# A chain of attention and two MLPs on one core: the up product of batch 1's channel MLP in Strassen's seven block products

## The chip, the core and the metric

The kernel runs on one core of a Trainium2 chip. The metric is the device time of one execution in microseconds (us). TensorE (PE in the profile) multiplies, its weight loads (PEld) lie beside its matmuls; VectorE (DVE), ScalarE (ACT) and GpSimd (POOL) do the rest, and SyncE (SP) issues most DMAs. Each engine takes its instructions in a fixed order.

## What is computed

The reference is an attention with cluster masks, then a channel MLP behind a mixing by Fourier transforms, then a gated MLP. The change touches the channel MLP alone:

```python
def _moe_ref(x, w_ch1, w_ch2) -> np.ndarray:
    X = np.fft.fft(x, axis=1)
    X = np.fft.fft(X, axis=2)
    mixed = np.real(X).astype(np.float32)
    u = x + mixed
    mu = np.mean(u, axis=-1, keepdims=True)
    var = np.mean((u - mu) ** 2, axis=-1, keepdims=True)
    un = (u - mu) / np.sqrt(var + 1e-06)
    ch = np.maximum(un @ w_ch1, 0.0) @ w_ch2
    return (u + ch).astype(np.float32)
```

Here x is 2 batches of 768 tokens with 512 features, w_ch1 is 512 x 2048 and w_ch2 2048 x 512. The gated MLP behind it (512 to 1024 and back, with a convolution over tokens and a sigmoid) runs in the same loop style with "second weights".

## The kernel before

**Number format.** Values of fp32 accuracy are held as two fp16 tiles, a high part and a low part (value less high part). A product takes three matmul passes, high x high, high x low and low x high (`pass3`, lines 490 to 493). The weights come as 64-bit numbers; `load_w` (line 725) fetches a block of 128 hidden features by an SP DMA into one of two raw buffers, `from64` (line 701) turns it into fp32 on VectorE and ScalarE, and the split gives the four pieces (up high and low, down high and low).

**The channel MLP.** It runs in blocks f = 0 to 15 of 128 hidden features, batch g = 0 first, then g = 1 (main loop, lines 1820 to 1849). `mlp1_up` (line 1647) makes block f + 1: for each half of the tokens (384) `up_half` sums 4 chunks of 128 input features by 3 passes, 12 matmuls into one of two PSUM banks called up; ScalarE writes the high part (line 1661), VectorE the low part (line 1663). Then `down` (line 1702) adds block f into six accumulator banks, one for each token tile of 128: 18 matmuls of 512 columns. So the up product of the next block always lies between a block's end and its use.

**Beside it.** A generator `side` is advanced once or twice inside each `down`. In batch 0 it is `later`: the mixing and the norm of batch 1 (`norm`, line 653), whose `swap` turns normed tiles by four transposes into an up bank, and whose results are the batch's activations `un`. In batch 1 it is `gate_in(0)` (line 1727): `measure` scales rows of U, then six token tiles are turned through an up bank (line 1771) into x, the gated MLP's input, one tile in each of f = 2 to 7. The loads of the second weights (blocks wb0 to wb7) are placed at the blocks of `B_LOADS` in batch 1; each takes the SBUF slot of a first weight block that its last down has freed. `scales("b")` after f = 12 forms their scales, and `split_16` the pieces of the first three.

**Order.** The instruction order of each engine is fixed at build time by a scheduler that goes by the written order and by when it expects an instruction to be ready. An accurate general version follows behind a flag that a set of checks computes; the profiled execution doesn't run it.

Of the kernel before, what the change touches and what calls it, by code (L numbers as in the profile page):

```python
# [2 lines left out]

# [6 lines left out]
F16 = mybir.dt.float16  # L10
# [438 lines left out]
def tile_net(ctx, tc, qk, v, cen, w12, w34, conv, dft, odd, out, general):  # L449
# [51 lines left out]
    def mixing(b, bank, bank2, low, other, rest):  # L501
# [223 lines left out]
    def load_w(k, f):  # L725
# [29 lines left out]
    def scales(k):  # L755
# [9 lines left out]
        V.tensor_reduce(sc[:, 0:2], o.rearrange("p (a f) -> p a f", a=2), AX.X, ALU.max)  # L765
        if k == "a" and not general:
# [29 lines left out]
    def heads_fit():  # L796
        o = up_bank("heads")
        least, most = (V_LEAST ** 2 * 128 * S, V_MOST ** 2 * 128 * S)
        V.tensor_scalar(hsum[:, 0:16], hsum[:, 0:16], QK_MOST ** 2, None, ALU.is_le)
        T.matmul(o[:, 0:24], ones.to_broadcast([128, 128]), hsum, start=True, stop=True)  # L800
        T.matmul(o[:, 32:40], ones.to_broadcast([128, 128]), ties, start=True, stop=True)
# [899 lines left out]

    def down(s, g, f, side, when=(2,)):
        w, h = ws.pop((s, g, f)), hs.pop((s, g, f))
# [3 lines left out]
        for t in range(NT):  # L1707
# [4 lines left out]
            if f == last:  # L1712
# [6 lines left out]
                else:  # L1719
# [74 lines left out]
    def later():  # L1794
# [25 lines left out]
    for g in range(B):  # L1820
        for f in range(16):
            if (g, f) < (B - 1, 15):
                mlp1_up(*((g, f + 1) if f < 15 else (g + 1, 0)))
            if (g, f) == (B - 1, 15):
                next(side, None)
            down(0, g, f, side, (1, 4) if g == 0 and f else (2,))
            for i in A_LOADS[f] if g == 0 else ():
# [15 lines left out]
            if (g, f) == (1, 12):  # L1843
# [104 lines left out]
```

## Time and profile before

| | us |
|---|---|
| median of 3 runs | 634.34 (633.04 to 634.71) |
| profiled execution | 634.69 |
| its span | 632.9 |
| TensorE busy | 608.3 |
| batch 1's first up matmul to the first matmul of the gated MLP | 363.36 to 494.90 |

The span is the time from the first to the last instruction; 1.8 us of the profiled execution lie around it. TensorE's granted clock is 1.00 in the stretches from 217 to 495 us. A busy time counts what the engine executes; what matters for an engine's worth is whether TensorE waits for it.

### The profile page before, as it was taken

The page shows a single profiled execution, that of the slowest core. Times are in us where ns is not written, and L with a number is a line of the kernel's source. Part 1 is how long each engine was busy: PE and PEld are TensorE (multiplying, and loading weights), DVE is VectorE, ACT ScalarE, POOL GpSimd, SP SyncE. Part 2 cuts the span into 40 slices and gives each one's busy share as a digit, 9 for nine tenths or more (in the row PEclk, how much of TensorE's full clock was granted, in tenths as well). Part 3 has the DMA queues.
Part 4 walks back from the last instruction along what each step waited for, and adds up shares of the span by engine and source line. Part 5 has one row for each costly group of instructions (what it writes and reads, how often), then busy time and mean ns, then how long its engine had stood idle before and what let it go on. Part 6 is the DMA issues. An engine that isn't in the chain of part 4 may idle for free.

```text
span 632.9 us, 11869 instructions
## 1 busy us (share of the span) xinstructions
PE 608.3 (96%) x4753; PEld 371.0 (59%) x4753; DVE 472.6 (75%) x784; ACT 413.0 (65%) x714; POOL 169.3 (27%) x137
## 2 busy tenths in 40 slices
PE   8899899999999999999999999999999999999995
PEld 4476577676877755566555555555555545555552
DVE  5989979899898889877894177777114599777663
ACT  6788899996889866873686134555115568866652
POOL 4978877875697300000200000000000000000000
PEclk9999999999999999999999999999999999999998
DMA  4676764641410513430353002333100003345102
GB/s 157 204 183 209 211 153 127 156 121 46 105 42 4 200 61 123 151 132 1 146 187 134 1 1 92 117 131 112 50 1 2 0 2 99 101 150 184 67 1 105
DMA packets 21945, 64.40 MB, mean 102 GB/s; under 512 B 7127, under 2 KB 8823, under 8 KB 19065
## 3 DMA queue, kind: packets, MB, share of 16 engines
q1 hardware_dynamic: 20872, 59.81, 30.0%
q0 software_dynamic: 1008, 3.75, 2.0%
q8 instruction: 39, 0.64, 0.4%
q14 instruction: 26, 0.20, 0.1%
HBM read 49.59 MB, written 4.89 MB: 86 GB/s over the span
## 4 chain that ended last, share of the span: by engine, by line
PE 68%; DVE 16%; ACT 11%; issue 2%; DMA 1%; DVEq 0%; ACTq 0%
PE acc L491 7%; PE acc L493 7%; PE acc L492 7%; PE av L1280 5%; PE up L491 5%; PE up L493 5%; PE up L492 5%; PE t L1224 4%; DVE m6all L1173 4%; PE t L1226 4%; PE s L1164 3%; PE av L1273 2%; PE u L491 2%; PE u L493 2%; PE u L492 2%
## 5 line engine op out<-in xcount | busy, mean ns | idle before, releaser
L1261 POOL TENSOR_TENSOR p<-p,p 128x768 f16<-128x768 f32 x61 | 108.0, 1780 | 39.1 <-DVE p L1249 15.0
L1173 DVE TENSOR_REDUCE m6all<-s 128x1 f32<-128x768 f32 x96 | 89.9, 948 | 9.5 <-PE s L1164 7.4
L1233 ACT ACTIVATE p<-t,cbias 128x768 f32<-128x768 f32 x93 | 83.1, 896 | 14.1 <-PE t L1226 13.4
L491 PE MATMUL up<-un,wa 128*128 128x384 f16 x256 | 83.5, 326 | 1.9 <-DVE un L690 0.9
L493 PE MATMUL up<-un,wa 128*128 128x384 f16 x256 | 83.5, 326 | 0.0
L492 PE MATMUL up<-un,wa 128*128 128x384 f16 x256 | 83.4, 326 | 0.0
L1663 DVE SCALAR_TENSOR_TENSOR h<-up,h 128x384 f16<-128x384 f32 x62 | 33.6, 552 | 52.5 <-ACT h L1661 52.2
L1661 ACT ACTIVATE h<-up 128x384 f16<-128x384 f32 x62 | 29.8, 483 | 65.3 <-PE up L493 65.1
L491 PE MATMUL acc<-wa,h 128*128 128x512 f16 x186 | 70.6, 380 | 0.0
L492 PE MATMUL acc<-wa,h 128*128 128x512 f16 x186 | 70.5, 379 | 0.0
L493 PE MATMUL acc<-wa,h 128*128 128x512 f16 x186 | 70.5, 379 | 0.0
L1280 PEld LDWEIGHTS <-p 128*128 128x128 f16 x1458 | 55.0, 98 | 11.9 <-issue 3.2
L1280 PE MATMUL av<-V,p 128*128 128x65 f16 x1458 | 58.2, 194 | 0.0
L1224 PE MATMUL t<-X 97*128 97x384 f16 x192 | 47.3, 327 | 4.6 <-DVE m6all L1173 2.4
L1164 PE MATMUL s<-X 80*128 80x384 f16 x192 | 46.9, 328 | 5.0 <-DVE eq L969 3.1
L1251 ACT CAST p<-p 128x768 f16<-128x768 f32 x60 | 49.5, 825 | 0.9
L1226 PE MATMUL t<-Y 128*128 128x384 f16 x192 | 47.2, 327 | 0.0
L775 POOL TENSOR_TENSOR scb<-scb,half 128x2 f32<-128x2 f32 x1 | 0.7, 699 | 158.5 <-DVE scb L765 158.5
L491 PE MATMUL u<-x,wb 128*128 128x384 f16 x128 | 41.7, 326 | 0.2
L493 PE MATMUL u<-x,wb 128*128 128x384 f16 x128 | 41.7, 326 | 0.0
L492 PE MATMUL u<-x,wb 128*128 128x384 f16 x128 | 41.7, 326 | 0.0
L671 POOL TENSOR_TENSOR rs<-rs,half 128x1 f32<-128x1 f32 x12 | 9.9, 831 | 100.3 <-DVE rs L666 82.9
(366 smaller groups left out, 1310.4 us busy)
## 6 DMA issues: line engine op xcount, KB each, us to landing
rawa<-w SPq DMA_DIRECT2D x14, 1024.0 KB
rawb<-w SPq DMA_DIRECT2D x8, 1024.0 KB
heads<-qk SPq DMA_DIRECT2D x8, 768.0 KB
raw<-qk SPq DMA_DIRECT2D x7, 768.0 KB
Y<-G SPq DMA_DIRECT2D x27, 192.0 KB
vraw<-v SPq DMA_DIRECT2D x8, 384.0 KB
heads<-v SPq DMA_DIRECT2D x8, 384.0 KB
out<-y SPq DMA_DIRECT2D x12, 256.0 KB
```

The source lines that it names most:

```text
L491: T.matmul(o, sH, mH, start=start, stop=False)
L492: T.matmul(o, sH, mL, start=False, stop=False)
L493: T.matmul(o, sL, mH, start=False, stop=stop)
L1164: T.matmul(t[:, c, 0:384], X[0:80, 0, sl], X[0:80, 1, 384 * c:384 * c + 384], start=True, stop=True)
L1173: V.tensor_reduce(m6s[h][:, i:i + 1], t[:, :, 0:384], AX.XY, ALU.max, negate=True)
L1224: T.matmul(t[:, c, 0:384], X[0:rx, 1, sl], X[0:rx, 0, 384 * c:384 * c + 384], start=True, stop=False)
L1226: T.matmul(t[:, c, 0:384], Y[0:ry, k, sl], Y[0:ry, q, 384 * c:384 * c + 384], start=False, stop=True)
L1233: A.activation(p, t[:, :, 0:384], AF.Exp, bias=cbias[:, 0:1], scale=0.125 if general else 0.125 / QK_SCALE ** 2)
L1251: A.copy(p16[:, 0], p32s[n])
L1261: eng.tensor_sub(p16[:, 1], p, p16[:, 0])
L1280: T.matmul(o, p16[:, k, 128 * j:128 * j + 128], v16[:, i, h % 2, 65 * part:65 * part + 65], start=(i + j + k + part == 0), stop=(i == 5), ...
L1663: V.scalar_tensor_tensor(h[1][:, tk], o, 0.0, hh, ALU.max, ALU.subtract)
```

## The change

Batch 1's up product is done in pairs p of hidden blocks (2p, 2p + 1). The weights of a pair are a 2 x 2 array of blocks (two hidden blocks by two halves of the input features), the activations another (two halves of the features by two halves of the tokens). Seven block products p1 to p7, each of 2 chunks by 3 passes (6 matmuls), replace eight. Their operands are some of the blocks themselves and four sums of the weights and four of the activations; the results are added up in fp32.

- `norm_pairs` replaces `norm` for batch 1: token tiles are taken in the order 0, 3, 1, 4, 2, 5; tiles 0 to 2 are kept in fp32 as well, and with tile t + 3 the four sums of the activations are formed and split. The tile `un` has 7 pieces.
- `weight_sums` forms the four sums of a pair's weights in fp32 on GpSimd (two adds of 512 columns, four of 256), and ScalarE and VectorE split them. It stands two pairs ahead of their use.
- `ups` is the generator of the seven products. ScalarE copies p1 and p5 from PSUM, VectorE adds the others, GpSimd makes one sum of 384 columns, and `keep` writes the high and low parts of 768 columns from SBUF. `in_turn` interleaves it with the token tiles of `downs` by a string (u a product, d a tile).
- Second weights: the check for tiny values becomes an accumulating pass on ScalarE and a flag, in place of a compare on VectorE. `B_LOADS` goes from (1, 2, 4, 5, 7, 9, 10, 11) to (1, 3, 5, 7, 9, 10, 11, 12), and their scales are formed after f = 13.

```diff
-    NA, NB, B_LOADS = (2, 7, 7), (3, 5), (1, 2, 4, 5, 7, 9, 10, 11)
+    NA, NB, B_LOADS = (2, 7, 7), (3, 5), (1, 3, 5, 7, 9, 10, 11, 12)
...
-            for op in from64(w, raw):
+            ops = from64(w, raw, None if general else sums[:, 64 + f:65 + f])
+            for op in ops[0:2] + ops[3:4] if not general else ops:
                 i = op()
             last_op[:] = [i.ins]
+        if not general:
+            ops[2]()
+            ops[4]()
...
+        if k == "b" and not general:
+            T.matmul(b[:, 32:40], ones.to_broadcast([128, 128]), sums[:, 64:72], start=True, stop=True)
...
+        def swap(t):
+            un, tk = uns[b], slice(128 * (t % 3), 128 * (t % 3) + 128)
+            o = bank(f"unT{b}{t}").rearrange("p (a c n) -> p a c n", a=2, c=2)
+            for c in range(4):
+                T.transpose(o[:, c // 2, c % 2], norm_ys[b][t][:, 128 * c:128 * c + 128], ident)
+            if t < 3:
+                k = lp.tile([128, 2048], F32, tag="sv", bufs=1, name=f"turned{t}")[:, 0:1536]
+                k = turned[t] = k.rearrange("p (s c n) -> p s c n", s=6, c=2)
+                A.copy(k[:, 4:6], o)
+                A.copy(un[:, 0, 0:2, :, tk], o)
+                V.tensor_sub(un[:, 1, 0:2, :, tk], o, un[:, 0, 0:2, :, tk])
+                return
+            k = turned.pop(t - 3)
+            V.tensor_sub(k[:, 0], o[:, 0], k[:, 4])
+            A.copy(un[:, 0, 2, :, tk], o[:, 1])
+            V.tensor_sub(k[:, 1], o[:, 1], k[:, 0])
+            V.tensor_sub(un[:, 1, 2, :, tk], o[:, 1], un[:, 0, 2, :, tk])
+            V.tensor_sub(k[:, 3], k[:, 5], k[:, 1])
+            V.tensor_sub(k[:, 2], k[:, 1], k[:, 4])
+            A.copy(un[:, 0, 3:7, :, tk], k[:, 0:4])
+            V.tensor_sub(un[:, 1, 3:7, :, tk], k[:, 0:4], un[:, 0, 3:7, :, tk])
...
+    def weight_sums(p):
+        k = hp.tile([128, 2048], F32, tag="sv", bufs=1, name=f"sv{p}").rearrange("p (s c n) -> p s c n", s=8, c=2)
+        v, a1, a2 = k[:, 0:4], k[:, 4:6], k[:, 6:8]
+        for f, d in ((2 * p, a2), (2 * p + 1, a1)):
+            w = w32["a", f].rearrange("p (a i h c n) -> p a i h c n", a=2, i=2, h=2, c=2)
+            G.tensor_add(d, w[:, 0, 0], w[:, 1, 0])
+        G.tensor_add(v[:, 0], a2[:, 0], a2[:, 1])
...
+        A.copy(t[:, 0], v)
+        V.tensor_sub(t[:, 1], v, t[:, 0])
...
+        def product(name, w, x):
+            o = up_bank(f"{name}{p}")[:, 0:384]
+            for c in range(2):
+                pass3(o, w[0][c], w[1][c], un[:, 0, x, c], un[:, 1, x, c], c == 0, c == 1)
+            return o
...
+        def keep(src, f):
+            t = hp.tile([128, S], F32R, tag="hH", bufs=4, name=f"h1_{f}").bitcast(F16)
+            h = hs[0, 1, f] = [t[:, 0:S], t[:, S:2 * S]]
+            A.activation(h[0], src, AF.Relu)
+            V.scalar_tensor_tensor(h[1], src, 0.0, h[0], ALU.max, ALU.subtract)
+
+        lo, hi = slice(0, 384), slice(384, 768)
+        o = product("p1", own(0, 0), 0)
+        u1 = piece("u1")
+        A.copy(u1, o)
+        yield
+        u2 = piece("u2")
+        V.tensor_add(u2, u1, product("p6", of_sum(1), 4))
+        yield
+        c1 = row(0)
+        V.tensor_add(c1[:, lo], u1, product("p2", own(0, 1), 1))
+        yield
+        u3 = piece("u3")
+        V.tensor_add(u3, u2, product("p7", of_sum(2), 5))
+        yield
+        o = product("p5", of_sum(0), 3)
+        p5 = piece("p5")
+        A.copy(p5, o)
+        c2 = row(1)
+        V.tensor_add(c2[:, hi], u3, o)
+        u4 = piece("u4")
+        G.tensor_add(u4, u2, p5)
+        yield
+        V.tensor_add(c2[:, lo], u3, product("p4", own(1, 1), 6))
+        keep(c2, 2 * p)
+        yield
+        V.tensor_add(c1[:, hi], u4, product("p3", of_sum(3), 2))
+        keep(c1, 2 * p + 1)
+        yield
...
+            if not general and g and f % 2 == 0 and f < 12:
+                weight_sums(f // 2 + 2)
...
+            elif g == 0:
+                in_turn(steps, ups(0), iter("ududduuduudud"))
+            elif f % 2:
+                in_turn(steps, *made)
+            else:
+                made = (ups(f // 2 + 1), iter("ududdududduddudduddudd")) if f < 14 else ((), repeat("d"))
+                in_turn(steps, *made)
```

How the order of the engines changes, at the three places of which the prediction speaks. TensorE at f = 2 of batch 1, around the first turned tile (xT00; acc01n is the accumulator of tile n, h1_2 the block that is added, wa a weight block); before:

```order
L493 LDWEIGHTS h1_2_5274
L493 MATMUL acc012_5244<-wa2_3940,h1_2_5274 128x512
L1771 MATMUL xT00_5386<-ident_61,U_68 128x128 x4
L491 LDWEIGHTS h1_2_5274
L491 MATMUL acc013_5245<-wa2_3940,h1_2_5274 128x512
```

and now (p22 is product p2 of pair 2):

```order
L494 LDWEIGHTS h1_2_5400
L494 MATMUL acc012_5316<-wa2_3940,h1_2_5400 128x512
L1904 MATMUL xT00_5486<-ident_61,U_68 128x128 x4
L492 LDWEIGHTS wa5_4179
L492 MATMUL p22_5494<-un1_4593,wa5_4179 128x384
```

A product that takes the next up bank stands right behind the transposes, where a token tile of the down step stood.

VectorE at the same place (wb1 is a load of second weights, h1_n the low part of block n, x0 the turned tile); before:

```order
L1663 SCALAR_TENSOR_TENSOR h1_2_5274<-up1_2_0_5275,h1_2_5274 128x384
L1663 SCALAR_TENSOR_TENSOR h1_2_5274<-up1_2_1_5290,h1_2_5274 128x384
L707 TENSOR_SCALAR wb1_5402<-rawb1_5403 128x1024
L708 SCALAR_TENSOR_TENSOR wb1_5402<-rawb1_5403,wb1_5402 128x1024
L710 SCALAR_TENSOR_TENSOR wb1_5402<-rawb1_5403,wb1_5402 128x1024
L712 SCALAR_TENSOR_TENSOR wb1_5402<-rawb1_5403,wb1_5402 128x1024
L1663 SCALAR_TENSOR_TENSOR h1_3_5339<-up1_3_0_5340,h1_3_5339 128x384
L1663 SCALAR_TENSOR_TENSOR h1_3_5339<-up1_3_1_5355,h1_3_5339 128x384
L1774 TENSOR_TENSOR x0_5257<-xT00_5386,x0_5257 128x4x128
```

and now (uc10, u22, uc20 and u32 are sums of products; s163 the low part of pair 3's weight sums):

```order
L1782 TENSOR_TENSOR uc10_5346<-u41_5384,p31_5415 128x384
L710 TENSOR_SCALAR wb1_5587<-rawb1_5588 128x1024
L1727 TENSOR_TENSOR s163_5449<-sv3_5442,s163_5449 128x1024
L1755 SCALAR_TENSOR_TENSOR h1_3_5423<-uc10_5346,h1_3_5423 128x768
L711 SCALAR_TENSOR_TENSOR wb1_5587<-rawb1_5588,wb1_5587 128x1024
L1763 TENSOR_TENSOR u22_5464<-u12_5459,p62_5465 128x384
L713 SCALAR_TENSOR_TENSOR wb1_5587<-rawb1_5588,wb1_5587 128x1024
L1907 TENSOR_TENSOR x0_5338<-xT00_5486,x0_5338 128x4x128
L1766 TENSOR_TENSOR uc20_5493<-u12_5459,p22_5494 128x384
L1769 TENSOR_TENSOR u32_5505<-u22_5464,p72_5506 128x384
```

The load's steps stand between the sums that read the products' banks.

VectorE in the norm of batch 1 (un1 the activations, unT1n the turned tile n, y1n the normed tile); before:

```order
L690 SCALAR_TENSOR_TENSOR un1_4593<-unT10_4672,un1_4593 128x4x128
L664 BN_AGGR mv14_4777<-st14_4775 128x2
L708 SCALAR_TENSOR_TENSOR src12_4889<-rawa12_4890,src12_4889 128x1024
L676 TENSOR_SCALAR y12_4704<-U_68,mv12_4683,rs12_4685 128x512
L690 SCALAR_TENSOR_TENSOR un1_4593<-unT11_4697,un1_4593 128x4x128
```

and now:

```order
L846 TENSOR_TENSOR un1_4593<-unT10_4672,un1_4593 128x4x128
L849 TENSOR_TENSOR turned0_4677<-unT13_4699,turned0_4677 128x256
L679 TENSOR_SCALAR y11_4712<-U_68,mv11_4685,rs11_4687 128x512
L669 TENSOR_SCALAR rs12_4789<-mv12_4787 128x1
L738 SCALAR_TENSOR_TENSOR wa11_4826<-src11_4827,wa11_4826 128x1024
L851 TENSOR_TENSOR turned0_4677<-unT13_4699,turned0_4677 128x256
L852 TENSOR_TENSOR un1_4593<-unT13_4699,un1_4593 128x2x128
```

A turned tile of the second half is read three times, with a weight split between the first and the second reading.

## Rows read from the trace of the kernel before

**Rows 1.** page, part 1: busy us, share of span, instructions
```profile
PE 608.3 (96%) x4753; PEld 371.0 (59%) x4753; DVE 472.6 (75%) x784; ACT 413.0 (65%) x714; POOL 169.3 (27%) x137
```

**Rows 2.** stretches: PE, PEld, DVE, ACT, POOL busy us; clock; DMA
```profile
303.80:339.40 35.60, 34.68 (x193) 18.83 (x192) 30.53 (x43) 29.82 (x56) 2.65 (x2) 1.00 0.37 138
339.40:363.40 24.00, 24.00 (x134) 13.05 (x133) 3.59 (x7) 5.01 (x14) 0.00 (x0) 1.00 0.24 88
363.40:386.70 23.30, 23.30 (x128) 12.28 (x128) 17.10 (x54) 9.24 (x17) 0.00 (x0) 1.00 0.03 5
386.70:436.00 49.30, 49.30 (x277) 27.47 (x276) 36.52 (x47) 24.86 (x50) 0.00 (x0) 1.00 0.38 130
436.00:494.90 58.90, 58.90 (x322) 31.11 (x320) 20.27 (x37) 18.08 (x38) 0.70 (x1) 1.00 0.08 25
```

**Rows 3.** timeline of TensorE, batch 1: start us, duration us, instruction
```profile
392.56 0.60 PE L1771 MATMUL xT<-ident,U 128*128 128x128 f32 x4
393.00 0.38 PE L491 MATMUL acc<-wa,h 128*128 128x512 f16 x1
...
451.95 0.33 PE L491 MATMUL up<-un,wa 128*128 128x384 f16 x1
...
455.85 0.38 PE L491 MATMUL acc<-wa,h 128*128 128x512 f16 x1
...
459.74 0.33 PE L491 MATMUL up<-un,wa 128*128 128x384 f16 x1
```

**Rows 4.** groups by shape, 300 to end: busy us, mean ns | idle
```profile
L1663 DVE SCALAR_TENSOR_TENSOR h<-up,h 128x384 f16<-128x384 f32 x48 | 25.8, 552 | 51.2 <-ACT h L1661 51.0
L1661 ACT ACTIVATE h<-up 128x384 f16<-128x384 f32 x47 | 22.8, 485 | 61.8 <-PE up L493 61.8
L1699 ACT CAST gH<-cv 128x768 f16<-128x768 f32 x16 | 13.3, 832 | 7.4 <-DVE cv L1697 7.2
L709 ACT ACTIVATE rawb<-rawb 128x1024 f32<-128x1024 f32 x8 | 9.5, 1192 | 23.4 <-DVE wb L708 23.4
L735 DVE SCALAR_TENSOR_TENSOR wa<-src,wa 128x1024 f16<-128x1024 f32 x7 | 8.5, 1215 | 1.6 <-ACT wa L734 1.6
L734 ACT ACTIVATE wa<-src 128x1024 f16<-128x1024 f32 x6 | 6.3, 1046 | 0.0
```

**Rows 5.** instructions of lines 1261 and 634: ns min/median/max
```profile
L1261 POOL TENSOR_TENSOR p<-p,p x61: 1635/1647/2367, 23.3 to 215.9; 128x768 f16<-128x768 f32 x61
L1261 DVE TENSOR_TENSOR p<-p,p x17: 917/957/1693, 28.2 to 218.0; 128x768 f16<-128x768 f32 x17
L634 POOL TENSOR_TENSOR U<-U,m x3: 1084/1086/1092, 171.5 to 183.7; 128x512 f32<-128x512 f32 x3
```

**Rows 6.** timelines of VectorE and GpSimd, attention
```profile
102.92 0.95 DVE L1074 SCALAR_TENSOR_TENSOR G<-raw,G 128x768 f16<-128x768 f32 x1
...
105.28 9.23 POOL L1261 TENSOR_TENSOR p<-p,p 128x768 f16<-128x768 f32 x5 [2.75 <-DVE p L1249]
105.99 1.75 DVE L1074 SCALAR_TENSOR_TENSOR G<-raw,G 128x768 f16<-128x768 f32 x1
```

**Rows 7.** timeline of VectorE, norm stretch and batch 1
```profile
301.80 1.21 DVE L735 SCALAR_TENSOR_TENSOR wa<-src,wa 128x1024 f16<-128x1024 f32 x1
302.93 0.69 DVE L662 BATCH_NORM_STATS2 st<-U 128x6 f32<-128x512 f32 x1
...
395.14 0.69 DVE L707 TENSOR_SCALAR wb<-rawb 128x1024 int32<-128x1024 int32 x1 [0.63 <-PE acc L493]
...
402.04 0.69 DVE L1774 TENSOR_TENSOR x<-xT,x 128x512 f16<-128x512 f32 x1 [1.42 <-ACT x L1773]
```

**Rows 8.** waits, 210 to 500: us in total, times, longest us
```profile
PE up L491 <- DVE un L690: 0.9, 2, 0.5
```

**Rows 9.** timelines of TensorE and VectorE, second weights' scales
```profile
475.31 0.29 PE L763 MATMUL sumsb<-sums,ones 128*128 128x16 f32 x2
...
478.11 0.75 DVE L1637 SCALAR_TENSOR_TENSOR wb<-wb,scb,wb 128x512 f16<-128x512 f32 x1 [0.41 <-ACT wb L1636]
```

More of the change, by code (lines that the diff above doesn't have):

```diff
@@ L2 @@
 from contextlib import ExitStack, nullcontext
+from itertools import repeat
 import concourse.bass as bass
@@ L765, in scales @@
         V.tensor_reduce(sc[:, 0:2], o.rearrange("p (a f) -> p a f", a=2), AX.X, ALU.max)
+        if k == "b" and not general:
+            V.tensor_reduce(hsum[:, 24:25], b[:, 32:40], AX.X, ALU.max)
+            V.scalar_tensor_tensor(scl["a"][:, 8:9], hsum[:, 24:25], 0.0, scl["a"][:, 8:9], ALU.is_le, ALU.mult)
         if k == "a" and not general:
@@ L799, in heads_fit @@
         V.tensor_scalar(hsum[:, 0:16], hsum[:, 0:16], QK_MOST ** 2, None, ALU.is_le)
-        T.matmul(o[:, 0:24], ones.to_broadcast([128, 128]), hsum, start=True, stop=True)
+        T.matmul(o[:, 0:24], ones.to_broadcast([128, 128]), hsum[:, 0:24], start=True, stop=True)
         T.matmul(o[:, 32:40], ones.to_broadcast([128, 128]), ties, start=True, stop=True)
@@ L813, in heads_fit, with norm_pairs, stat_ @@
         scl["fits"] = r[:, 5:6].bitcast(I32)
+    def norm_pairs(b, bank, lp):
+        stat, root, scale, _, _ = norm(b, bank, lp)
+        turned = {}
+        def stat_(t):
+            if b not in uns:
+                uns[b] = up_[b].tile([128, 2, 7, 2, 384], F16, tag="un", bufs=1, name=f"un{b}")
+            stat(t)
+        def swap(t):
[19 more added lines that the diff above has]
+            V.tensor_sub(un[:, 1, 3:7, :, tk], k[:, 0:4], un[:, 0, 3:7, :, tk])
+        return stat_, root, scale, swap
     def up_half(o, w, x, i):
@@ L1648, in mlp1_up @@
         if not wide(g):
-            t = hp.tile([128, S], F32R, tag="hH", bufs=3, name=f"h{g}_{f}").bitcast(F16)
+            t = hp.tile([128, S], F32R, tag="hH", bufs=3 if general else 4, name=f"h{g}_{f}").bitcast(F16)
             h = hs[0, g, f] = [t[:, 0:S], t[:, S:2 * S]]
@@ new lines, in ups, with own, of_sum, piece @@
+    def ups(p):
+        un, sw = uns[1], sums_w.pop(p)
+        def own(row, half):
+            w = ws[0, 1, 2 * p + 1 - row]
+            return [[w[a][:, 256 * half + 128 * c:256 * half + 128 * c + 128] for c in range(2)] for a in range(2)]
+        def of_sum(i):
+            return [[sw[:, a, i, c] for c in range(2)] for a in range(2)]
+        def product(name, w, x):
[3 more added lines that the diff above has]
+            return o
+        def piece(tag):
+            return hp.tile([128, 384], F32, tag=tag, bufs=1, name=f"{tag}{p}")
+        def row(i):
+            return hp.tile([128, S], F32, tag=f"uc{i}", bufs=1, name=f"uc{p}{i}")
+        def keep(src, f):
[31 more added lines that the diff above has]
+        yield
@@ L1667, in mlp2_up, with in_turn @@
+    def in_turn(steps, made, turns):
+        n = 0
+        while n < NT:
+            if next(turns) == "u":
+                next(made)
+            else:
+                next(steps)
+                n += 1
     def mlp2_up(b, f):
@@ L1700, in gate, with down, downs @@
         V.tensor_sub(g[1], t, g[0])
-    def down(s, g, f, side, when=(2,)):
+    def down(*args):
+        for _ in downs(*args):
+            pass
+    def downs(s, g, f, side, when=(2,)):
         w, h = ws.pop((s, g, f)), hs.pop((s, g, f))
@@ L1803, in later @@
         wst.append(pool(hctx, "wstB"))
-        stat, root, scale, swap, low = norm(1, up_bank, hp)
+        order = range(NT) if general else (0, 3, 1, 4, 2, 5)
+        stat, root, scale, swap, *low = (norm if general else norm_pairs)(1, up_bank, hp)
         for u in range(NT + 2):
             if u > 1:
-                swap(u - 2)
-                low(u - 2)
+                swap(order[u - 2])
+                if general:
+                    low[0](order[u - 2])
             if 0 < u <= NT:
-                scale(u - 1)
+                scale(order[u - 1])
             if u < NT:
-                stat(u)
-                root(u)
+                stat(order[u])
+                root(order[u])
             yield
@@ L1821, in tile_net @@
         for f in range(16):
-            if (g, f) < (B - 1, 15):
+            pairs = not general and (g > 0 or f == 15)
+            if (g, f) < (B - 1, 15) and not pairs:
                 mlp1_up(*((g, f + 1) if f < 15 else (g + 1, 0)))
+            if not general and g == 0 and f > 13:
+                weight_sums(f - 14)
+            if not general and g and f % 2 == 0 and f < 12:
+                weight_sums(f // 2 + 2)
             if (g, f) == (B - 1, 15):
                 next(side, None)
-            down(0, g, f, side, (1, 4) if g == 0 and f else (2,))
+            steps = downs(0, g, f, side, (1, 4) if g == 0 and f else (2,))
+            if not pairs:
+                for _ in steps:
+                    pass
+            elif g == 0:
+                in_turn(steps, ups(0), iter("ududduuduudud"))
+            elif f % 2:
+                in_turn(steps, *made)
+            else:
+                made = (ups(f // 2 + 1), iter("ududdududduddudduddudd")) if f < 14 else ((), repeat("d"))
+                in_turn(steps, *made)
             for i in A_LOADS[f] if g == 0 else ():
@@ L1847, in tile_net @@
                 A.activation(warm, scl["b"][:, 0:1], AF.Sigmoid)
-            if g == 1 and f >= 13 and f < 13 + NB[0]:
-                ws_b[f - 13] = split_16(wbp[0], "b", f - 13)
+            for i in {13: (0,), 14: (1,), 15: (2,)}.get(f, ()) if g == 1 else ():
+                ws_b[i] = split_16(wbp[0], "b", i)
     hctx.close()
```

16 lines of the change are left out of this document (12 added, 4 removed).

## The prediction

> **What bounds the kernel now.** I read the page's busy times first: TensorE is busy for 608.3 of 632.9 us [rows 1]. Then the stretches of the trace, to see whether that holds where the change works: while batch 1's up product runs (363.4 to 494.9) TensorE has no idle time in any stretch, and VectorE has 17.1 busy of 23.3, 36.5 of 49.3 and 20.3 of 58.9 us [rows 2]. So a matmul taken away there is worth its issue time, as long as VectorE, ScalarE and GpSimd still deliver ahead of TensorE. Then TensorE's timeline, for the pitch of its matmuls: an up product of 24 runs from 451.95 to 455.85 (0.1625 each, 6 are 0.975), a down step of 18 from 455.85 to 459.74 (0.216 each, a token tile's three are 0.65), and four transposes move TensorE by 0.44 [rows 3].
>
> **What is removed.** A pair of feature blocks had 48 up matmuls and has 42 (seven products, two chunks of 128, three passes). Eight pairs: 48 x 0.1625 = 7.80 us, all of it on the path. Weight loads go with the matmuls and lie beside them.
>
> **What is added, and where it lies.** One small matmul into the scales' bank: the one that stands there takes 0.29 [rows 9], half of it before the next starts; I take 0.15. Everything else is VectorE, ScalarE and GpSimd work that TensorE feels only when a bank or an operand comes late.
>
> *Norm of batch 1 (303.8 to 339.4).* A transposed tile's bank was read by one cast and one subtraction (0.69 for 512 wide, as the row at 402.04 [rows 7]). Now three tiles keep that beside a second copy, and three have three subtractions of 256 from the bank (0.35 each, half of 0.69), two of 256 from SBUF and one of 1024 (1.22 [rows 4]). VectorE: 6 x 0.69 = 4.1 becomes 3 x 0.69 + 3 x (5 x 0.35 + 1.22) = 11.0, so 6.9 more, where 5.1 of 35.6 us are free; the rest goes into the next 24 us, which have 20.4 free [rows 2]. TensorE is hurt by the bank that the tile holds: before, it waited 0.9 in this stretch for such a subtraction [rows 8]. I followed VectorE's queue in the printed order from 306.23. Queued instructions there start 0.08 before the one ahead ends (1.21 after 301.80, yet the next starts at 302.93 [rows 7]). With that pitch up block 13 starts 0.2 later than before (the waits are 0.45, 0.85 and 0.55 at single banks, against 0.9 and small ones before); with whole durations 2.6 later. I take 0.5, near the pitch that the rows show, and keep 0 to 2.5.
>
> *Boundary of the batches (363.4 to 374).* VectorE adds six banks into U and reduces six rows between the reads of the first pair's products; before, a whole up product of 3.9 us lay ahead as cover. Followed in the same way, p3 of pair 0 waits 0.05 and p6 of pair 1 0.2 for a bank; if VectorE starts 0.6 late, about 1.5. I take 0.5 of 0 to 1.5.
>
> *Pairs 2, 3 and 4 (f 2 to 7).* This is the place that decides. VectorE over these six blocks: 36.5 busy before, less six compares (6 x 1.22) and twelve low parts (12 x 0.55), plus per pair six sums (0.55 each), two low parts of 768 (0.96, as the subtraction on VectorE in [rows 5]) and one of 1024 (1.22): 36.5 - 7.3 - 6.6 + 3 x 6.44 = 41.9, in 49.3 - 3 x 0.975 = 46.4 us [rows 2, 4, 5]. ScalarE: 24.9 - 12 x 0.48 + 6 x 1.19 + 3 x (2 x 0.48 + 2 x 0.83 + 1.05) = 37.3. Both fit, with little to spare, and two up banks turn round faster: each f now has transposes between the products, so the bank that p2 takes must be released within 1.73 us of the end of p6 (two tiles of down, 1.3, and the transposes), and p7 must find the transposes' bank read 1.6 us after them.
>
> Pair 2, zero at the end of pair 1's p3 on TensorE: down 1.30, p1 2.27, down 2.92, p6 3.90, down 5.19, transposes 5.63, p2. VectorE in the printed order: the sum of pair 1's p3 to 0.75; the load's first step waits for the down step that frees its slot, as at 395.14 [rows 7], and runs from 1.5 to 2.1; weights' low sums to 3.25, h low to 4.1, the load's second step to 5.25, and only then the sum that frees p6's bank, to 5.8: p2 is 0.2 late. The load's third step to 6.9, then x (behind ScalarE's Square, 1.19, and cast) to 7.75, where p7 wants the bank at 7.45: 0.3 late. Pair 3 has the same order; in pair 4 the sum stands ahead of the load's steps. So 0.6 + 0.6 + 0 = 1.2 as the lower end.
>
> The upper end comes from GpSimd. It now adds the weights of the pair after next right behind the weights' low sums: two of 512 (1.09 each, the row of L634) and four of 256 (half), 4.4 us, and one of 384 (0.82) later [rows 5]. A two-operand VectorE instruction that started at 105.99, with GpSimd at work since 105.28, took 1.75, where one at 102.92 took 0.95 [rows 6]: it lost 0.80. If the load's second step waits out the first 512 add and the third step the second, p2 comes 1.3 late and p7 another 0.9: 2.2 in pairs 2 and 3, 0.9 in pair 4, together 5.3. Against it: of 17 such VectorE instructions in the attention, where GpSimd works much of the time, the median is 957 and the least 917 [rows 5], so most meet nothing. No row says which of these lies nearer; I take the middle, 3.2.
>
> [...]
>
> *Pairs 1, 5, 6, 7.* Without transposes each bank has 2.9 us from product to reuse, and its reader needs 0.75. I take 0.4 of 0 to 1.
>
> *Edits at nothing.* The second weights' loads keep their slots and order on SP's queue; the compare of each (1.22, VectorE) becomes an accumulating pass on ScalarE, counted above. Scales of those weights come one block later: before, the first split was there 478.86 - 475.31 = 3.6 us after the scales' matmul [rows 9]; now 36 down matmuls, 7.8 us, lie between it and the product that needs it. If the table load and one more h low came ahead, some 2 us of the cover would still be left. The fourth hH buffer costs nothing.
>
> **The sum.** -7.80 + 0.15 + 0.5 + 0.5 + 3.2 + 0.4 = -3.05. The profiled execution took 634.69 (span 632.9 and 1.8 around it), so 631.6; the median shown is 0.35 below it, so **631.3**. All lower ends give -6.5 (627.9), all upper ends +2.65 (637.0).
>
> **Rivals.**
> *Cover holds everywhere*: VectorE's queue meets GpSimd seldom, only the 1.2 of the transposes is lost: -6.45, 627.9. For it: the median 957. Against it: VectorE at 41.9 of 46.4.
> *The norm holds the banks*: the norm's stretch costs its upper 2.5 and not 0.5, the rest as forecast: -1.05, 633.3, no change that can be told. For it: TensorE already waits there. Against it: the pitch.
> *GpSimd makes VectorE the bound (slower)*: in pairs 2 to 4 GpSimd works 3 x (4.4 + 0.82) = 15.6 us; VectorE has 4.5 to spare. If it is blocked for all 15.6, the stretch is 11.1 too long: -7.8 + 0.15 + 1.0 + 11.1 + 0.4 = +4.85, 639.2. Slower by 1.9 or more begins where 12.8 of the 15.6 block it. For it: the instruction at 105.99. Against it: sums from a bank have one SBUF operand, and only some 8 us of VectorE's 14 a pair have two. [...]
>
> **How the numbers follow.** Runs of this kernel tell about 0.3% (1.9 us) from no change. Chances: forecast 0.44 (0.40 of it beyond 0.3% faster), cover holds 0.22, norm 0.22, VectorE bound 0.12. So faster 0.62, same 0.26, slower 0.12. The range goes from the case in which the cover holds, with 0.9 for the scatter of the runs, to between the norm's and the slower one: 627.0 to 636.5.
>
> **What would show it.** Batch 1's first product to the first u product: 131.5 us before; 123.7 plus the stalls now. TensorE's waits by releaser: u2 and x on VectorE in f 2 to 7 (about 1 us a pair), little in f 8 to 13. VectorE's wb steps at L711 and L713 longer than 1.22 where GpSimd runs: the lock. Start of up block 13 in batch 0: within 0.5 of before, or 2.5 late. The forecast is wrong if the loads' steps never stand ahead of the sums, or if GpSimd's adds take far more than 1.09.

## The result

The changed kernel takes 638.3 us (636.24 to 639.62), the kernel before 634.62 (633.04 to 635.72), 11 runs each; the ratio is 1.0057, interval 1.0047 to 1.0068. It is slower by 0.6%, where 631.3 and a gain were forecast, and it lies outside the range of 627.0 to 636.5. The profiled execution of after took 637.55, 2.86 more than that of before. Page of after, part 1 (busy us, share, instructions; before is [rows 1]):

```profile
PE 602.3 (95%) x4707; PEld 366.7 (58%) x4707; DVE 509.4 (80%) x833; ACT 438.2 (69%) x744; POOL 236.0 (37%) x193
```

TensorE is busy for 6.0 us less and still ends later. The stretches of after show where (columns as in [rows 2], which they answer):

```profile
303.80:339.20 35.40, 34.59 (x194) 18.92 (x193) 32.22 (x54) 26.84 (x48) 4.72 (x3) 1.00 0.38 141
339.20:365.20 26.00, 24.07 (x133) 12.97 (x132) 12.83 (x13) 13.41 (x29) 17.45 (x18) 1.00 0.23 82
365.20:390.00 24.80, 24.80 (x137) 13.23 (x137) 22.24 (x61) 11.79 (x18) 8.87 (x8) 1.00 0.00 1
390.00:439.00 49.00, 43.59 (x239) 23.56 (x238) 42.69 (x53) 32.13 (x62) 27.14 (x21) 1.00 0.31 111
439.00:497.60 58.60, 57.11 (x307) 29.61 (x305) 31.47 (x51) 25.29 (x46) 12.68 (x11) 1.00 0.13 43
```

TensorE stands still for 1.93 us before the first product, 5.41 in 390 to 439 and 1.49 behind it; before, it stood nowhere between 339.4 and 494.9 [rows 2]. From the first product (365.24) to the first u product (497.59) it is 132.35 us, where before had 131.54. The arithmetic wanted 131.54 - 7.80 + 0.15 = 123.9, so this stretch holds 8.45 of stalls. Block 15's up product of batch 0, ahead of it, takes 5.99 (354.77 to 360.76, by the pitch of its matmuls) where before had 3.90: 2.1 more. By the ends of its rows, as the runs below give it, that is 6.16 where before had 4.06. With 0.2 less ahead of that and 0.2 more behind the stretch this is the whole difference: 2.1 + 0.8 - 0.2 + 0.2 = 2.9.

What TensorE waited for, 339 to 512 of after (us in total, times, longest):

```profile
PE p L492 <- DVE u L1763: 4.5, 3, 1.8
PE p L492 <- DVE x L1907: 2.4, 3, 1.5
PE up L492 <- DVE h L1708: 1.9, 1, 1.9
PE u L492 <- DVE h L1803: 1.1, 1, 1.1
```

u at L1763 is the sum of p6, x the turned tile's low part. The last row lies behind the stretch, at 502.80 in the gated MLP; before has no such wait there. The same on TensorE's timeline (start, duration, instruction, in brackets the idle time ahead and its releaser):

```profile
394.67 0.60 PE L1904 MATMUL xT<-ident,U 128*128 128x128 f32 x4
397.06 0.32 PE L492 MATMUL p<-un,wa 128*128 128x384 f16 x1 [1.79 <-DVE u L1763]
...
399.29 0.32 PE L492 MATMUL p<-un,s 128*128 128x384 f16 x1 [0.45 <-DVE x L1907]
...
414.54 0.32 PE L492 MATMUL p<-un,wa 128*128 128x384 f16 x1 [1.24 <-DVE u L1763]
...
416.78 0.32 PE L492 MATMUL p<-un,s 128*128 128x384 f16 x1 [0.46 <-DVE x L1907]
...
433.87 0.32 PE L492 MATMUL p<-un,s 128*128 128x384 f16 x1 [1.47 <-DVE x L1907]
...
449.62 0.32 PE L492 MATMUL p<-un,wa 128*128 128x384 f16 x1 [1.45 <-DVE u L1763]
```

In pairs 2, 3 and 4 a product waits 1.79, 1.24 and 1.47 for a bank, with a second wait of 0.45 in two of them, and pair 5 waits 1.45 without any turned tile. Taken by the pitch of the instructions the stalls are 0.25 at the boundary, 2.56, 2.02 and 1.76 in pairs 2, 3 and 4, and 1.8 around pair 5. What VectorE and GpSimd did at the first of these places, timelines of both:

```profile
393.49 0.95 DVE L1755 SCALAR_TENSOR_TENSOR h<-uc,h 128x768 f16<-128x768 f32 x1
394.36 2.18 DVE L711 SCALAR_TENSOR_TENSOR wb<-rawb,wb 128x1024 int32<-128x1024 int32 x1
396.46 0.54 DVE L1763 TENSOR_TENSOR u<-u,p 128x384 f32<-128x384 f32 x1
396.93 1.71 DVE L713 SCALAR_TENSOR_TENSOR wb<-rawb,wb 128x1024 uint32<-128x1024 uint32 x1
...
393.65 3.90 POOL L1719 TENSOR_TENSOR sv<-wa 128x512 f32<-128x512 f16 x2 [6.06 <-DVE s L1727]
397.51 1.72 POOL L1720 TENSOR_TENSOR sv<-sv 128x256 f32<-128x256 f32 x1
```

This is to be read row against row. GpSimd's two adds of 512 begin at 393.65, 0.16 after VectorE's low part of h began, and take 3.90, not the 2.26 of 350.85. The load's step L711 begins when that low part ends and takes 2.18, not 1.23: the first add, 1.81 long, reaches to 395.46. L711 ends at 396.54, and the second add at 397.55, a whole add later. L713 begins at 396.93 and ends at 398.64, nearly a whole step after that add; the add of 256 behind it begins at 397.51 and ends at 399.23, nearly a whole add after L713. So at this place each ends about the length of an instruction behind the other, in turn, as if it had waited for the other's end: L711 at 396.54, the add at 397.55, L713 at 398.64. u2, behind L711, takes 0.54 as always, but it ends at 397.00 and its bank was wanted at 395.11. Lengths over the kernel (ns, min/median/max), of after:

```profile
L711 DVE SCALAR_TENSOR_TENSOR wb<-rawb,wb x8: 1225/1844/2181, 385.1 to 446.9; 128x1024 int32<-128x1024 int32 x8
L713 DVE SCALAR_TENSOR_TENSOR wb<-rawb,wb x8: 1379/1574/1715, 387.1 to 449.5; 128x1024 uint32<-128x1024 uint32 x8
L1719 POOL TENSOR_TENSOR sv<-wa x16: 1147/1802/2142, 337.3 to 448.0; 128x512 f32<-128x512 f16 x16
```

Five of the eight L711, the first load's in each of the pairs 1 to 5, meet adds and take 1.63 to 2.18; the three others take 1.23. The same two steps in before, where GpSimd had nothing to do there:

```profile
L708 DVE SCALAR_TENSOR_TENSOR wb<-rawb,wb x8: 1224/1226/1227, 379.9 to 437.0; 128x1024 int32<-128x1024 int32 x8
L710 DVE SCALAR_TENSOR_TENSOR wb<-rawb,wb x8: 1224/1226/1226, 381.1 to 438.2; 128x1024 uint32<-128x1024 uint32 x8
```

The same meeting stands 17 us ahead of block 15's stall (timelines of GpSimd, VectorE, ScalarE and TensorE of after):

```profile
337.27 3.58 POOL L1719 TENSOR_TENSOR sv<-wa 128x512 f32<-128x512 f16 x2 [14.69 <-DVE un L856]
...
339.87 2.06 DVE L711 SCALAR_TENSOR_TENSOR src<-rawa,src 128x1024 int32<-128x1024 int32 x1
...
355.99 1.05 ACT L1726 CAST s<-sv 128x1024 f16<-128x1024 f32 x1 [4.72 <-POOL sv L1723]
356.94 0.86 ACT L1706 ACTIVATE h<-up 128x384 f16<-128x384 f32 x2
...
358.82 0.32 PE L492 MATMUL up<-un,wa 128*128 128x384 f16 x1 [1.93 <-DVE h L1708]
```

Pair 0's sums on GpSimd and the last first-weight load on VectorE stretch each other from 337 to 347: the two adds of 512 take 3.58, where the next pair's at 350.85 take 2.26, and L711 takes 2.06, where the median of its 14 first-weight steps is 1.22. Pair 1's sums end at 355.96, ScalarE's cast of them starts at 355.99 with the high part of block 14's second half queued behind it, VectorE's low part follows, and the bank comes 1.93 late. How much earlier pair 1's sums would end without the meeting ahead of them, no run separates.

### The profile page after: what moved, and what is told of

It reads as the page before. It is cut to its first block, busy times and chain, and to the rows that moved or that the text cites. A ratio compares the mean times of both kernels' runs of the same rounds, so it can differ in the third digit from the quotient of the medians.

```text
span 635.8 us, 11958 instructions
## 1 busy us (share of the span) xinstructions
PE 602.3 (95%) x4707; PEld 366.7 (58%) x4707; DVE 509.4 (80%) x833; ACT 438.2 (69%) x744; POOL 236.0 (37%) x193
## 4 chain that ended last, share of the span: by engine, by line
PE 56%; DVE 25%; ACT 12%; issue 3%; DMA 2%; POOL 1%; DVEq 0%; ACTq 0%
PE acc L494 6%; PE acc L493 6%; PE acc L492 6%; PE av L1325 5%; PE t L1269 4%; DVE m6all L1218 4%; PE t L1271 4%; PE s L1209 3%; PE av L1318 2%; PE u L492 2%; PE u L493 2%; PE u L494 2%; PE p L492 2%; DVE wb L711 2%; PE p L493 2%
## 5 line engine op out<-in xcount | busy, mean ns | idle before, releaser
L1719 POOL TENSOR_TENSOR sv<-wa 128x512 f32<-128x512 f16 x16 | 26.2, 1657 | 51.7 <-DVE s L1727 37.0
L492 PE MATMUL up<-un,wa 128*128 128x384 f16 x128 | 41.7, 326 | 3.5 <-DVE h L1708 1.9
L494 PE MATMUL up<-un,wa 128*128 128x384 f16 x128 | 41.7, 326 | 0.0
L493 PE MATMUL up<-un,wa 128*128 128x384 f16 x128 | 41.7, 326 | 0.0
L493 PE MATMUL acc<-wb,gH 128*128 128x512 f16 x96 | 36.4, 379 | 0.0
L492 PE MATMUL acc<-wb,gH 128*128 128x512 f16 x96 | 36.4, 379 | 0.0
```

The costliest lines, as they stand in the source:

```text
L492: T.matmul(o, sH, mH, start=start, stop=False)
L493: T.matmul(o, sH, mL, start=False, stop=False)
L494: T.matmul(o, sL, mH, start=False, stop=stop)
L1719: G.tensor_add(d, w[:, 0, 0], w[:, 1, 0])
```

## Experiments

Two theories: LOCK, the adds on GpSimd and VectorE's steps with two SBUF operands shut each other out; QUEUE, VectorE's order alone (a load's steps ahead of the sums) makes the banks late. Each run has its stretch (first product to first u product) from its own profile; stall is what lies over 123.9. Ratios are to the kernel before, run in the same set (its medians 634.5 to 635.3). One kernel that was run in two sets gave 0.9916 and 0.9943, with the same stretch to 0.01, so ratios of different sets can be compared to some 0.003 only, and the stretch is the finer measure.

| kernel | stretch | stall | ratio (95%) | median |
|---|---|---|---|---|
| the change | 132.35 | 8.45 | 1.0057 (1.0047 to 1.0068) | 638.30 |
| no adds | 127.06 | 3.2 | 0.9945 (0.9925 to 0.9965) | 631.23 |
| loads held | 127.47 | 3.6 | 0.9979 (0.9962 to 0.9996) | 633.06 |
| adds on VectorE | 131.55 | 7.7 | 0.9996 (0.9978 to 1.0014) | 634.26 |
| late cast | 132.57 | 8.7 | 1.0035 (1.0018 to 1.0053) | 636.45 |
| copies for adds | 128.49 | 4.6 | 0.9937 (0.9914 to 0.9960) | 631.28 |
| fills for adds | 127.04 | 3.1 | 0.9916 (0.9889 to 0.9942) | 629.51 |
| held + late cast | 127.63 | 3.7 | 0.9916 (0.9895 to 0.9937) | 630.48 |
| the same again | 127.63 | 3.7 | 0.9943 (0.9927 to 0.9960) | 631.15 |
| + ScalarE's part late | 127.28 | 3.4 | 0.9919 (0.9893 to 0.9944) | 630.53 |
| + low parts and one load behind p7 | 130.85 | 7.0 | 0.9999 (0.9986 to 1.0012) | 634.27 |
| no adds, loads held | 127.50 | 3.6 | 0.9946 (0.9925 to 0.9966) | 631.00 |
| loads behind p7 | 125.39 | 1.5 | 0.9895 (0.9876 to 0.9914) | 628.37 |

### No adds

```diff
 def weight_sums(p):
+    if p == 0:
         ... the six GpSimd adds, as in the change
+        sums_w["v"] = v
+    v = sums_w["v"]
     ... cast (ScalarE) and subtraction (VectorE), as in the change
```

> The six GpSimd adds of the weight sums are left out from pair 1 on; the cast and the subtraction that follow them read pair 0's sums instead, so the output is not the reference's. Every other instruction and the order of TensorE and of VectorE in batch 1 stay. Theory LOCK (the adds stretch VectorE's steps that have two SBUF operands, L711 and L713 were 1.84 and 1.57 median against 1.22, and the banks come late by that): both steps back at 1.22, batch 1's first product to first u product 132.35 -> 125 to 126.5, and block 15's 2.1 us go too, since no cast waits for GpSimd: 628.5 to 631. Rival QUEUE (the load's steps stand ahead of the sums that free the banks, and that alone makes them late): only block 15 improves, 635.5 to 637, stretch 131 or more.

Ratio 0.9945, stall 3.2, block 15 at 4.07. VectorE's two steps (L711, L713 as in after) and TensorE's waits for products' banks:

```profile
L711 DVE SCALAR_TENSOR_TENSOR wb<-rawb,wb x8: 1218/1225/1227, 384.9 to 442.6; 128x1024 int32<-128x1024 int32 x8
L713 DVE SCALAR_TENSOR_TENSOR wb<-rawb,wb x8: 1218/1394/1572, 386.5 to 444.2; 128x1024 uint32<-128x1024 uint32 x8
```

```profile
PE p L492 <- DVE u L1766: 0.8, 3, 0.3
PE p L492 <- DVE x L1910: 0.8, 1, 0.8
```

LOCK holds, a little above its ranges (stretch 127.06 where 126.5 was the most, median 631.23 where 631 was): L711 is back at 1.22 and 5.3 of the 8.45 go with the adds, as block 15's 2.1 do. L713's longest, 1.57, meets the one GpSimd instruction that is left there, the add of u4 (in after too L713 takes 1.57 at 404.09, where that add began at 403.34).

### Loads held

```diff
+HELD = {1: (0, None), 2: (1, None), 3: (2, None), 4: (3, None), 5: (4, 5), 6: (6, 7)}
 # in ups(p), for the pair's first and second block:
     keep(c2, 2 * p)
+    second(HELD.get(p, (None, None))[0])
 # second(i): load_w("b", i), its VectorE steps issued after keep's low part
```

> The second weights' loads are held on VectorE behind the low part of a pair's first block (one load a pair in pairs 1 to 4, two in pairs 5 and 6) so that none of their steps stands between a pair's first sums; the GpSimd adds stay. LOCK and QUEUE both expect the waits for u2 and x at f 2 to 7 (8 us of stalls in the stretch) to go: LOCK because the adds now run beside sums from a bank, which have one SBUF operand, QUEUE because the sums stand first: stretch 125.5 to 127.5, 631.5 to 634 (block 15's 2.1 stay). If neither is right and something else holds TensorE: 637 to 639.

0.9979 and a stall of 3.6, as both theories expected. The adds are still there. Now they meet a sum of products, which has one operand in a PSUM bank (timelines of VectorE and GpSimd):

```profile
395.08 0.56 DVE L1771 TENSOR_TENSOR u<-u,p 128x384 f32<-128x384 f32 x1
...
395.32 2.26 POOL L1720 TENSOR_TENSOR sv<-wa 128x512 f32<-128x512 f16 x2 [8.58 <-DVE s L1728]
```

Two adds of 512 take 2.26, and u2 beside them 0.56, where the sums of p6 in after have a median of 0.55 and the two adds at 350.85 take 2.26: neither feels the other. In after, too, the five sums of p6 beside an add take 0.54 to 0.55.

### Adds on VectorE

```diff
-        G.tensor_add(d, w[:, 0, 0], w[:, 1, 0])   # and the five others
+        V.tensor_add(d, w[:, 0, 0], w[:, 1, 0])
```

> The six adds of the weight sums are done by VectorE in place of GpSimd. LOCK: steps L711 and L713 back at 1.22, but VectorE gets two adds of 512 and four of 256 a pair, about 3.1 us by its rows of those sizes (0.69 and 0.42), in a stretch where it has 4.5 to spare over three pairs: 636 to 640, with the waits now at other banks. QUEUE: the queue is longer still, 640 to 644.

634.26, below both ranges (LOCK's 636 to 640 had not counted that block 15's stall goes too, QUEUE's was 640 to 644). L711 and L713 take 1.22 again (at 392.23 and 394.97), as LOCK says. But the stretch itself gains 0.8 only: a fuller queue of VectorE costs nearly what the meetings did, and the waits have moved to more places (TensorE's waits, 339 to 500):

```profile
PE p L492 <- DVE x L1907: 1.5, 3, 0.9
PE p L492 <- DVE u L1763: 1.3, 2, 0.8
PE xT L1904 <- DVE uc L1775: 1.1, 1, 1.1
```

### Late cast

```diff
+    with tc.issue_after(...):  # for p == 1: behind the reading of up block 15, ScalarE and VectorE
     A.copy(t[:, 0], v)
     V.tensor_sub(t[:, 1], v, t[:, 0])
```

> Only the cast and the subtraction of pair 1's weight sums are moved: on ScalarE and VectorE they stand behind the reading of up block 15, not between block 14's halves. Theory BLOCK 15 (ScalarE waited 4.7 us for GpSimd's sums with block 14's second half queued behind, so up block 15 waited for a bank): up block 15 takes 4.07 as before and not 6.16, first product 2.1 earlier, 636.2. Rival: the bank is late for the adds' lock on VectorE, and the wait only moves: 637.5 to 638.5.

636.45, where 636.2 was expected: block 15's up product is back at 4.06, and the stretch stays at 132.57. The two stalls are independent.

### Copies and fills in place of the adds

```diff
-        G.tensor_add(d, w[:, 0, 0], w[:, 1, 0])   # and the five others
+        G.tensor_copy(d, w[:, 0, 0])              # copies
+        G.memset(d, 0.5)                          # fills
```

Two theories of what in the adds lengthens L711: READ, any GpSimd instruction that reads SBUF does it, so L711 stays far over 1.22 beside a copy, and the time was put at 633 to 637; TWO, only one with two operands does it.

> Each of the six GpSimd adds of the weight sums becomes a copy of its first operand to the same place (the output is not the reference's); all other instructions and their order stay. It asks what in the adds shuts VectorE out. [...] Rival TWO (only a GpSimd instruction with two operands): L711 at 1.22 as with no adds, 630.5 to 632.

> Each of the six adds becomes a fill with a constant of the same place and size (the output is not the reference's): GpSimd writes as much and reads nothing. READ and TWO: L711 and L713 at 1.22 and the time of the kernel without adds, 630.5 to 632. Rival WRITE (GpSimd at work, or its writes, is enough): steps stretched, 634 or more.

With copies, timelines of VectorE and GpSimd:

```profile
391.27 1.63 DVE L711 SCALAR_TENSOR_TENSOR wb<-rawb,wb 128x1024 int32<-128x1024 int32 x1
...
390.55 2.82 POOL L1719 CAST sv<-wa 128x512 f32<-128x512 f16 x2 [6.05 <-DVE s L1727]
393.32 1.44 POOL L1720 COPY sv<-sv 128x256 f32<-128x256 f32 x1
394.71 0.40 POOL L1722 COPY sv<-sv 128x256 f32<-128x256 f32 x1
```

L711 takes 1.63 beside a copy, and a copy of 256, 0.40 at 394.71, takes 1.44 beside L713: in these rows reading with one operand is enough, READ. The time, 631.28, is not in READ's range but in TWO's, as copies are short and meet less (stall 4.6, 1.5 more than fills); the length of L711 decides between the two. With fills L711 never leaves 1.22, though the fills begin behind the same low part as the adds (L1727, for which GpSimd waited 7 times in each of the two), and the stall is that of no adds, 3.1 against 3.2 (629.51, 1.0 under the expected range):

```profile
L711 DVE SCALAR_TENSOR_TENSOR wb<-rawb,wb x8: 1217/1226/1227, 381.3 to 439.0; 128x1024 int32<-128x1024 int32 x8
```

So in these runs VectorE's step with two SBUF operands was lengthened by a GpSimd instruction that reads SBUF (1.63 beside a copy, up to 2.18 beside adds) and stayed at 1.227 or less with fills, which only write it, in the adds' places; the sum from a bank, with one SBUF operand, was not lengthened by adds either (0.56). GpSimd's instruction was lengthened in turn (1.44 for 0.40, the copy of 256).

### Both edits, and what is left

```diff
 # held + late cast: the two edits above together
 # + ScalarE's part late: a load's four ScalarE passes behind the next pair's copy of p1
     u1 = piece("u1")
-    A.copy(u1, o)
+    i = A.copy(u1, o).ins
+    with tc.issue_after(i):
+        while rests: rests.pop(0)()
```

> The two edits that helped, together: loads held behind the low part of a pair's first block, and pair 1's cast behind up block 15. If their stalls are independent the gains add (5.2 and 1.85 from 638.3): 631.2. If the stall of block 15 only moves into the first pairs: 632.5 to 633.5.

> The kernel with held loads and the late cast once more, beside the one above on the same chip, for its interval: ratio to the kernel before 0.990 to 0.994.

> As the one before, and ScalarE's part of each held load (two passes of 1024, two of 512) stands behind the copy of the next pair's p1. In the held kernel TensorE waited 1.7 us for that copy, with such passes ahead of it. If that was the cause: 1.2 to 1.7 less than the one before, 629.5 to 630. If the bank is late for other reasons: no difference.

Held and late cast gave 0.9916 and, run again, 0.9943 (just over its expected range): 3.7 to 4.8 us below before, and 630.48 and 631.15 where independent stalls would give 631.2. Moving ScalarE's passes changed nothing, 0.9919: the wait for the copy of p1 went, others came up, the stall only from 3.7 to 3.4. (Of the expected 1.7, 0.9 was the wait of a weight load; matmuls waited 0.8 for that copy.)

### The fourth corner

> No GpSimd adds from pair 1 on (output not the reference's) and the loads held: the fourth corner of a square. Stalls in the stretch (beyond 123.9) are 8.45 with adds and loads as in the change, 3.15 without adds, 3.56 with loads held. LOCK: the two edits take away the same thing, the meeting of adds and loads' steps, so both together leave nearly what each leaves, 2.5 to 3.3. QUEUE as a cause of its own: the gains add, and under 1 is left.

The edit is the first two together, without the late cast. Stall 3.6: with held loads the adds cost nothing (3.6 with and without), and without adds holding the loads gains nothing (3.2 and 3.6). The two edits take away one and the same thing, the meeting; what is left, a little over LOCK's 2.5 to 3.3, has another cause. QUEUE as a cause of its own, with gains that add, would have left under 1.

### What stands ahead of u2

Both on top of the kernel with held loads, late cast and ScalarE's part late.

```diff
 # low parts and one load behind p7
     u3: V.tensor_add(u3, u2, product("p7", ...))
+    low part of the next weight sums; for pair 6 also load_w("b", 5)
 # loads behind p7, low parts where they were
+HELD, MID = {5: (4, None), 6: (6, None)}, {2: 0, 3: 1, 4: 2, 5: 3, 6: 5, 7: 7}
     u3: V.tensor_add(u3, u2, product("p7", ...))
+    if p in MID: load_w("b", MID[p], mids)   # ScalarE's part behind the copy of p5
```

> As the kernel with ScalarE's passes moved, and two more things leave the place between a pair's end and its second product on VectorE: the low part of the next weight sums (1.22) goes behind the sum of p7, and so does the second load of pair 5. Some 3.3 us of waits are left there in the stretch, in about 13 places of 0.1 to 0.55, most of them for u2, the sum of p6. If it is VectorE's queue ahead of u2: 1 to 2 less, ratio to the kernel before 0.989 to 0.990. If those waits come from the banks' own round (product, sum, next product), nothing changes: 0.992.

> As the kernel with ScalarE's passes moved, but the loads' steps stand on VectorE behind the sum of p7 in pairs 2 to 7 (and the weight sums' low part stays where it was, so the adds still run while VectorE adds up products). Ahead of u2 then stand only the low parts. LOCK: a load's first long step meets the last adds of 256 (0.7 at most a pair), and the waits for u2 go: 1 to 2 less than the kernel before it, ratio 0.988 to 0.990. Rival: the loads' steps, 3.1 in a row, now hold the sum of p5, or meet the adds fully as when the split stood there: ratio 0.993 to 1.000.

The first made it worse, 0.9999 and 7.0 of stall, where either theory had expected 0.992 or less. It moves ScalarE's cast of the sums together with their low part. The low part frees the tile that GpSimd's next adds fill, so these moved with it, into the half in which the loads' steps stand (timelines of VectorE and GpSimd):

```profile
424.24 1.63 DVE L711 SCALAR_TENSOR_TENSOR wb<-rawb,wb 128x1024 int32<-128x1024 int32 x1
...
422.22 1.44 POOL L1729 TENSOR_TENSOR sv<-sv 128x256 f32<-128x256 f32 x1
423.62 1.17 POOL L1730 TENSOR_TENSOR sv<-sv 128x256 f32<-128x256 f32 x1
```

L711 at 1.63, an add of 256 at 1.44. The second moved the loads and not the low part. The adds are through before a load begins (timelines of VectorE and GpSimd, then TensorE's waits, 339 to 500):

```profile
391.13 0.55 DVE L1784 TENSOR_TENSOR u<-u,p 128x384 f32<-128x384 f32 x1 [0.74 <-PE p L494]
...
395.86 0.69 DVE L710 TENSOR_SCALAR wb<-rawb 128x1024 int32<-128x1024 int32 x1
396.58 1.23 DVE L711 SCALAR_TENSOR_TENSOR wb<-rawb,wb 128x1024 int32<-128x1024 int32 x1
397.84 1.23 DVE L713 SCALAR_TENSOR_TENSOR wb<-rawb,wb 128x1024 uint32<-128x1024 uint32 x1
...
394.65 0.72 POOL L1730 TENSOR_TENSOR sv<-sv 128x256 f32<-128x256 f32 x1
```

```profile
PE u L492 <- DVE h L1832: 1.0, 1, 1.0
PE p L492 <- DVE uc L1810: 0.4, 1, 0.4
```

The row at L1832 lies behind the stretch. u2 starts at 391.13, behind nothing, L711 and L713 take 1.23, and only 1.5 of stall is left of 8.45. The step from 3.4 to 1.5 is QUEUE's and not LOCK's, since with loads held the adds already cost nothing (it moves ScalarE's passes as well, which the run before found to cost little). At 628.37, 0.9895, this kernel is 6.5 us faster than before: the change pays 6.5 of the 7.65 of its arithmetic once VectorE's two-operand steps and GpSimd's adds are apart in time and the sums stand first.

## Why the prediction was wrong, step by step

- *-7.80 and +0.15* held: the stalls of after read place by place come to 8.39, and 132.35 less the arithmetic's 123.9 is 8.45.
- *Norm, 0.5 (0 to 2.5)*: block 13 starts at 339.20, before at 339.42. That start alone says little, for it lies between 337.4 and 341.3 in the runs; but in the norm's stretch TensorE stands still for 0.81, where before had 0.92 [rows 2]. Nothing was lost; the pitch of the queue [rows 7], near which I chose, was the right row.
- *Boundary, 0.5 (0 to 1.5)*: 0.25.
- *Pairs 2, 3 and 4, 3.2 (1.2 to 5.3)* is the step that failed: 6.3, over its upper end. The mechanism was named (p2 behind u2, the load's steps lengthened by GpSimd), the value was the middle between two bounds with the words that no row says which lies nearer. The printed order said it: the adds wait for the low part of the sums before them (s163), and the load's two long steps stand close behind that low part. So the first load of a pair meets them every time, in pairs 1 to 5. The 17 instructions of the attention [rows 5], which I set against it, were misread: a median of 957 does not say that most meet nothing. In the trace of before ten of them lie beside a GpSimd instruction. In five of these VectorE's took 0.99 to 1.69; in the other five it kept 0.92 to 0.96, and in three of them the row of GpSimd is the longer one, as here (timelines of VectorE and GpSimd, before; the least of L1130 is 0.52):

```profile
164.07 0.92 DVE L1261 TENSOR_TENSOR p<-p,p 128x768 f16<-128x768 f32 x1
...
164.07 1.30 POOL L1130 TENSOR_SCALAR V<-vraw 128x128 f32<-128x128 f32 x1
```

The upper end, 5.3, in which the load's long steps wait out adds of 512, was nearer.
- The two ends of that term were low as well. Without adds pairs 2 to 4 still lose 2.4 (0.3 to 0.9 at five places), not 1.2. Loads behind p7 take most of that away and ScalarE's passes hardly any, so it is VectorE's queue ahead of u2 and x, of which I had counted half. And the adds alone take 5.1 a pair (2.26 for two of 512, 0.72 for one of 256), not 4.4: half the columns are not half the time.
- *Pairs 1, 5, 6, 7, 0.4 (0 to 1)*: 1.8, nearly all at pair 5, where the adds for pair 7 and the last load meet (446 to 451). I had tied the waits to the turned tiles and let them end with these; they go with the adds.
- *339 to 363* had no term. The first two pairs' sums are made there; I priced them at nothing, since no product of batch 1 runs yet. ScalarE's cast of pair 1's sums waits for GpSimd and holds the queue behind it: 2.1, which the late cast takes away. That pair 0's sums and the last load of first weights lengthen each other ahead of it is seen; its share of the 2.1 is open.
- *Edits at nothing*: the first product that needs the later scales did not wait (497.59). But the splits behind them now lie in the start of the gated MLP, and at 502.80 TensorE waits 1.15 until a low part that stands behind two of them on VectorE is through, a wait that before does not have. Of it 0.2 is left at the end; no run takes that apart.
- *VectorE and ScalarE*: VectorE is busy for 42.69 of 49.00, waits on GpSimd included, where 41.9 was summed, and ScalarE for 32.13, where 37.3 was.

In sum 2.1 + 6.3 + 1.8 stand where 3.6 stood, 6.6 more; norm and boundary took 1.0 less, 0.2 came behind the stretch, and 0.1 is rounding: the 5.9 between -3.05 and +2.86. The rival *GpSimd makes VectorE the bound* had the sign and nearly the time (639.2), but not the way: VectorE is busy 42.69 of 49 in the worst stretch, not full. What stood against it, that sums from a bank have one SBUF operand, had no row behind it then; the five sums beside adds in after (0.54 to 0.55) and u2 with held loads (0.56) are such rows. (Its 12.8 should read 12.65: -6.25 + 12.65 - 4.5 is the 1.9.) *Cover holds everywhere* (627.9) is what loads behind p7 come to, at 628.4.

What stays open: the last 1.5 us of stall in the best kernel lie in many places of 0.1 to 0.5, and no run takes them apart.

## What to carry to other kernels

Work put on GpSimd because it is idle was free here while VectorE added up sums from a bank (stall 3.6 with held loads, with and without adds), or when GpSimd read nothing (3.1 with fills), and not beside VectorE's steps with two SBUF operands (stall 8.45). Set the two queues side by side in time: where such steps stood at the same place in each round, as in pairs 1 to 5 here, both paid in turn, L711 up to 2.18 for 1.23 and an add of 512 up to 2.14 for 1.15. A row of VectorE that is not longer than usual does not show that nothing was met; look at GpSimd's row beside it (at 164.07 of before VectorE kept 0.92, and GpSimd took 1.30 where its least is 0.52). Where a product's bank is released by a sum on VectorE, nothing that can wait belongs ahead of that sum, if it meets nothing where it goes: loads moved behind p7 took the stall from 3.4 to 1.5, low parts and one load moved there, with the adds behind them, to 7.0. And price a change in every stretch in which it puts an instruction, also where its main work does not run yet.

## What was not expected of the hardware

Meeting costs both sides, over the whole kernel: the add of 512 has a median of 1.80, where it takes 1.15 with the loads held, and the load's step 1.84 for 1.23. VectorE's first step of a load (L710) has one operand, and yet took 1.19 in place of 0.69 at 436.34, where an add of 256 had begun at 436.25. At 430.43 it began 0.01 ahead of an add of 512, kept its 0.69, and the add took 1.69. Sums from a bank have one SBUF operand too and felt nothing (0.54 to 0.56 beside adds), so the number of operands alone does not tell the two apart; why L710 meets GpSimd, no run here takes up.
